# Identity and masks of an attention kernel made on GpSimd and VectorE, padding not loaded, and the order planned anew

## The chip, the cores and the metric

The program runs on one core of one Trainium2 chip. The metric is device time of one execution in microseconds; the time before is the median of three runs, 335.76 us. PE is the matrix engine TensorE, DVE is VectorE, ACT is ScalarE, POOL is GpSimd, and SP is SyncE, which here only issues DMAs.

## What is computed

Two steps follow each other, for 4 batches, 4 heads, 1088 positions. The first is an attention with a feature map (products of two projections of 8 values each, so 64 features a head). The second is a gated feed-forward block that mixes positions with a 1088 x 1088 matrix.

```python
def phi(x):
    a = np.einsum('rd,bhsd->bhsr', S1, x)
    b = np.einsum('rd,bhsd->bhsr', S2, x)
    return np.einsum('bhsi,bhsj->bhsij', a, b).reshape(*x.shape[:-1], r * r)
q_p, k_p = (phi(q), phi(k))
kv = np.einsum('bhsf,bhsd->bhfd', k_p, v)
z = np.sum(k_p, axis=2)
num = np.einsum('bhsf,bhfd->bhsd', q_p, kv)
den = np.einsum('bhsf,bhf->bhs', q_p, z)[..., None] + 1e-06
x = num / den                                   # heads side by side: 128 columns
...
h = np.maximum(x @ w_in, 0.0)                   # 1024 columns, halves u and v
v_n = (v - mean(v)) / sqrt(var(v) + 1e-06)
v_s = np.einsum('ts,bsd->btd', w_spatial, v_n) + b_spatial[None, :, None]
out = (u * v_s) @ w_out
```

## The kernel before

Positions are padded to 9 tiles of 128, in three groups of three. fp32 numbers are split into a high and a low part (wTh and wTl of w_spatial, vh and vl of the normed v, xh and xl of x, wih and wil of w_in), and three products of such parts make one full product. `S1`, `S2`, `w_in` and `w_out` arrive as fp64 bit patterns and are turned into fp32 by the seven VectorE steps of `from_f64`.

The program is a list of operations (`op`), each with its engine, its tiles and a planned cost. `Order.schedule` puts them in a row for each engine from tables of numbers: `LEADS` (how much earlier than needed an operation is due), `FORCE` (which engines may take an operation), `FIRST` (loads that go first), `T_MAIN` and `PACE` (when the products of each batch are due). In places where the plan leaves PE free it puts in products of zeros (`fill`). Each engine then works strictly in its row's order.

Batch 0 has a path of its own (`attention0`) that has to come before anything else: the table `sk` of S1 and S2 goes through `from_f64` on DVE; the keys kt are projected with it on PE; ACT copies half of that (ka), DVE multiplies the halves into features (kp), four times 128x768 for the three groups of keys and the first of queries; PE sums features and values into pu; DVE masks that by head into kd0 (L665 before); PE turns the query features with an identity matrix (L688), forms num and den (L702), DVE divides (L706 to L709), PE turns the result (L716), ACT and DVE split it into xh and xl, and `hidden_v` makes the normed v from it. Then `main` runs the large products with w_spatial (L956, L958, L965) over four column blocks d, three position chunks c, and nine tiles kt.

Before the change one array, `idn`, is loaded into `ident`: 128 columns of identity, 2 columns `in_turn` that tell the head of a pair for the kd of batches 1 to 3 (L762), and 4 columns by head for kd0 (L665). The seven steps that make `sk` need no part of it.

Of the kernel before, what the change touches and what calls it, by code (L numbers as in the profile page):

```python
# [9 lines left out]
F32 = mybir.dt.float32  # L10
# [9 lines left out]
P = 128  # L20
# [26 lines left out]
T_MAIN = (39.0, 143.0, 197.0, 292.0)  # L47
PACE = (1.145, 0.898, 1.306, 1.037)
STRETCH = 1.64
FORCE = {'abs': ['ACT'], 'norm0': ['ACT', 'DVE'], 'vl0': ['DVE'], 'v90': ['ACT'], 'W0': ['DVE'], 'W1': ['DVE'], 'W2': ['POOL']}  # L50

FIRST = ('wt21', 'wt20', 'wt02', 'wt12', 'wt11', 'wt40', 'wt01', 'wt22')
# [6 lines left out]
ON_ACT = ()  # L59
ADD_UP = 187  # L60

AHEAD = 90000
TURN = 125

SLACK = {'PE': 5, 'ACT': 29, 'DVE': 91, 'POOL': 5000, 'SP': 5000}
FILL, FILL_TO, FILL_SPARE = 224, 50.0, 150

COLD_TO, COLD = 6800, 2

FILLS = ((7000, 460, 260), (8200, 300, 100), (1e9, FILL, -FILL_SPARE))  # L70
FIRST_RATE, LOW_DELAY = 0.18, 4.4
# [48 lines left out]
class Order:  # L120
# [235 lines left out]
def c_mm(n, k=1):  # L356
    return k * max((n + 11.8) / 2.25, 111)


@with_exitstack  # L360
def tile_kernel(ctx: ExitStack, tc: tile.TileContext, kT, qT, vA, sks, idn, wT, w_in, w_out, bsp, out):
# [86 lines left out]
    def from_f64(x32, raw, n):  # L448

        def w(i):
            return raw[:, :2 * n].bitcast(U32).rearrange("p (n w) -> p w n", w=2)[:, i]

        def x():
            return x32[:, :n]

        def xb():
            return x32[:, :n].bitcast(U32)

        def step(cost, f, r, w):
            op("DVE", cost, lambda: f(nc.vector), r=r, w=w, sh=True)

        c2, c1 = c_dve2(n), c_dve(n)

        if n > NSK:
            op("ACT", c_act(n), lambda: nc.scalar.activation(x(), w(1).bitcast(F32), AF.Abs), r=[raw], w=[(x32, "x")], sh=True, alts=[("DVE", c2, lambda: nc.vector.tensor_scalar(out=xb(), in0=w(1), scalar1=0x7FFFFFFF, scalar2=None, op0=ALU.bitwise_and))], kind="abs")
        else:
            step(c2, lambda v: v.tensor_scalar(out=xb(), in0=w(1), scalar1=0x7FFFFFFF, scalar2=None, op0=ALU.bitwise_and), [raw], [(x32, "x")])
        step(c2, lambda v: v.tensor_scalar(out=x(), in0=x(), scalar1=EXP_LO, scalar2=EXP_HI, op0=ALU.max, op1=ALU.min), [], [(x32, "x")])  # L470
# [9 lines left out]
        step(c1, lambda v: v.tensor_tensor(out=x(), in0=x(), in1=ev(), op=ALU.add), [(x32, "e")], [(x32, "x")])  # L480
# [651 lines left out]
```

## Time and profile before

| what | us |
|---|---|
| median of three runs (335.5 to 335.83) | 335.76 |
| profiled execution, its own time | 335.18 |
| its span | 333.4 |
| DVE busy | 197.4 |
| ACT busy | 157.9 |
| POOL busy | 56.9 |

The span runs from the program's first instruction to its last; 1.8 us of the profiled execution's time lie around it. Times on a row of the timeline are the start from the span's start, then the duration. A timeline merges equal instructions that follow each other, with their count. In square brackets stands how long the engine was idle just before, and what ended that. In a row of windows, the figures are busy time and instructions of each engine in the stretch, then PE's granted clock, the busy share of the DMA engines and what they moved.

### The profile page before, as it was taken

The numbers are of one execution on the slowest core, as the hardware profiler recorded it, in microseconds if no ns is written. First come the engines' busy times: TensorE is split into PE (matmuls) and PEld (weight loads), VectorE is DVE, ScalarE is ACT, GpSimd is POOL, SyncE is SP. The second block draws the span as 40 slices with busy tenths as digits, with TensorE's granted clock in tenths as the row PEclk, the third lists the DMA queues.
The fourth block names the chain that finished last, engine by engine and source line by source line (L and its number), as shares of the span: only waits on it lengthen the run. The fifth ranks groups of instructions, "written<-read, shape, count | busy, mean of one in ns | idle before, by whom it ended". The sixth has DMA issues, their size and how long they took to land.

```text
span 333.4 us, 6019 instructions
## 1 busy us (share of the span) xinstructions
PE 326.5 (98%) x2304; PEld 315.4 (95%) x2304; DVE 197.4 (59%) x448; ACT 157.9 (47%) x367; POOL 56.9 (17%) x68
## 2 busy tenths in 40 slices
PE   7999999999999999999999999999999999999996
PEld 7878979999999999999999999999999999999995
DVE  4899997355889972779984232255992473121221
ACT  2589667532668652556563232336651542121212
POOL 1000105472423106401313200131000000000000
PEclk9999999999999999999999999999999999999999
DMA  7901379667310175501037110310000100000001
GB/s 210 342 20 48 109 191 316 127 135 194 86 44 27 29 123 95 118 0 48 22 54 119 42 46 0 50 31 0 3 0 2 40 27 2 0 2 0 0 2 68
DMA packets 17747, 23.09 MB, mean 69 GB/s; under 512 B 2486, under 2 KB 17462, under 8 KB 17718
## 3 DMA queue, kind: packets, MB, share of 16 engines
q1 hardware_dynamic: 17718, 22.71, 27.0%
q8 instruction: 18, 0.29, 0.4%
q14 instruction: 11, 0.09, 0.1%
HBM read 13.78 MB, written 2.23 MB: 48 GB/s over the span
## 4 chain that ended last, share of the span: by engine, by line
PE 86%; DVE 7%; ACT 2%; DMA 2%; SPq 1%; issue 1%; DVEq 0%; ACTq 0%
PE sp L956 20%; PE sp L965 18%; PE sp L958 17%; PE sd L404 3%; PE sd L405 3%; PE sd L406 3%; PE pu L404 2%; PE po L405 2%; PE pu L406 2%; PE pu L405 2%; PE sp L967 2%; PE po L406 2%; PE po L404 2%; PE sd L614 2%; DMA v<-in_vA 2%; PE sd L568 1%
## 5 line engine op out<-in xcount | busy, mean ns | idle before, releaser
L956 PE MATMUL sp<-wTh,vh 128*128 128x362 f32 (+4 forms) x414 | 135.9, 328 | 0.0
L958 PE MATMUL sp<-wTh,vl 128*128 128x362 f32 (+4 forms) x368 | 120.4, 327 | 0.0
L965 PE MATMUL sp<-wTl,vh 128*128 128x362 f32 (+4 forms) x368 | 119.0, 328 | 0.7 <-DVE wTl L533 0.7
L956 PEld LDWEIGHTS sp<-wTh,vh 128*128 128x128 f32 x414 | 78.0, 188 | 1.0
L965 PEld LDWEIGHTS sp<-wTl,vh 128*128 128x128 f32 x368 | 69.3, 188 | 1.6 <-DVE wTl L533 1.3
L958 PEld LDWEIGHTS sp<-wTh,vl 128*128 128x128 f32 x368 | 69.4, 188 | 0.7
L993 DVE TENSOR_TENSOR u<-sp,u 128x362 f32<-128x362 f32 (+3 forms) x36 | 18.4, 510 | 45.1 <-PE sp L967 44.6
L484 ACT CAST g<-u 128x362 fp32r<-128x362 f32 (+3 forms) x34 | 16.4, 482 | 38.8 <-DVE u L993 38.6
L783 DVE RECIPROCAL c<-c 128x384 f32<-128x384 f32 (+1 forms) x9 | 21.7, 2416 | 10.5 <-ACT c L781 10.5
L417 POOL TENSOR_TENSOR r<-pl,r 128x384 fp32r<-128x384 f32 (+1 forms) x18 | 17.6, 982 | 59.1 <-ACT r L484 55.1
L809 DVE BATCH_NORM_STATS2 st<-vt 128x6 f32<-128x512 f32 x36 | 24.3, 689 | 4.9 <-ACT vt L807 4.8
L414 DVE TENSOR_TENSOR g<-u,g 128x362 fp32r<-128x362 f32 (+3 forms) x34 | 19.8, 581 | 11.0 <-ACT g L484 10.9
L807 ACT ACTIVATE vt<-sd 128x512 f32<-128x512 f32 x36 | 21.4, 600 | 9.1 <-PE sd L406 8.4
L749 POOL TENSOR_TENSOR pl<-pl,pl 128x384 f32<-128x384 f32 (+1 forms) x18 | 17.6, 984 | 35.7 <-DMA pl<-abT 32.0
L417 POOL TENSOR_TENSOR r<-c,r 128x384 fp32r<-128x384 f32 (+1 forms) x9 | 10.0, 1116 | 75.5 <-ACT r L484 75.5
L885 ACT CAST vh<-vt 128x384 fp32r<-128x384 f32 x36 | 17.2, 511 | 11.3 <-PE sp L956 4.9
L948 ACT ACTIVATE u<-pu 128x362 f32<-128x362 f32 (+3 forms) x36 | 16.4, 455 | 11.0 <-PE pu L406 10.8
L993 DVE TENSOR_TENSOR kp<-sp,kp 128x424 f32<-128x424 f32 x10 | 6.0, 600 | 26.1 <-PE sp L967 26.1
L887 DVE TENSOR_TENSOR vl<-vt,vh 128x384 fp32r<-128x384 f32 (+1 forms) x36 | 17.3, 504 | 1.4 <-ACT vh L885 1.3
L404 PE MATMUL pu<-xh,wih 128*128 128x362 f32 (+4 forms) x48 | 15.9, 331 | 0.0
L406 PE MATMUL pu<-xh,wil 128*128 128x362 f32 (+4 forms) x48 | 15.8, 329 | 0.0
L405 PE MATMUL pu<-xl,wih 128*128 128x362 f32 (+4 forms) x48 | 15.7, 328 | 0.0
(166 smaller groups left out, 540.2 us busy)
## 6 DMA issues: line engine op xcount, KB each, us to landing
pl<-in_wT SPq DMA_DIRECT2D x18, 166.0 KB, 3.7
v<-in_vA SPq DMA_DIRECT2D x12, 198.0 KB, 4.0
kt<-in_kT SPq DMA_DIRECT2D x12, 192.0 KB, 3.2
pl<-abT SPq DMA_DIRECT2D x12, 192.0 KB, 3.9
pl<-in_wT SPq DMA_DIRECT2D x9, 212.0 KB, 4.7
c<-in_qT SPq DMA_DIRECT2D x9, 192.0 KB, 2.8
pl<-abT SPq DMA_DIRECT2D x24, 72.0 KB, 2.3
pl<-abT SPq DMA_DIRECT2D x6, 160.0 KB, 3.7
```

The source lines that it names most:

```text
L404: nc.tensor.matmul(o, ah, bh, start=start, stop=False)
L405: nc.tensor.matmul(o, ah, bl, start=False, stop=False)
L406: nc.tensor.matmul(o, al, bh, start=False, stop=stop)
L414: return lambda: nc.vector.tensor_tensor(out=o(), in0=a(), in1=bb(), op=ALU.subtract)
L417: return lambda: nc.gpsimd.tensor_tensor(out=o(), in0=a(), in1=bb(), op=ALU.subtract)
L783: op("DVE", 135 + 6.3 * n, lambda x32=x32, n=n: nc.vector.reciprocal(out=x32[:, :n], in_=x32[:, :n]), w=[x32])
L807: op("ACT", c_act(512, True), lambda pv=pv, t=t: nc.scalar.activation(vt[:, t], pv.ap, AF.Relu), r=[pv], w=[(vt, t)])
L809: op("DVE", 690, lambda stats=stats, t=t: nc.vector.bn_stats(out=stats.ap, in_=vt[:, t]), r=[(vt, t)], w=[stats])
L956: nc.tensor.matmul(sp[:, :cw], vh[:, kt], wTh[:, kt, cs], start=(kt == 0), stop=False)
L958: nc.tensor.matmul(sp[:, :cw], vl[:, kt], wTh[:, kt, cs], start=False, stop=False)
L965: nc.tensor.matmul(sp[:, :cw], vh[:, kt], wTl[:, kt, cs], start=False, stop=False)
L993: op("DVE", c_dve(cw), lambda: nc.vector.tensor_tensor(out=u.ap, in0=sp[:, :cw], in1=u.ap, op=ALU.mult), r=[sp], w=[u], lead=LEAD[1])
```

## The change

The array `idn` goes. POOL now fills `ident` with ones and keeps the diagonal by an `affine_select`; it makes `by_head` with three small memsets; DVE makes `in_turn` by a sum over the columns of `ident`. The padding is no longer loaded: the last 64 columns of the third group of batch 0's keys are set to zero on POOL, those of its queries are copied on POOL from the 64 columns before them, and the two loads shrink from 384 to 320 columns. `FORCE` now names engines tile by tile, and all tables of the plan have new numbers.

```diff
-T_MAIN = (39.0, 143.0, 197.0, 292.0)
-PACE = (1.145, 0.898, 1.306, 1.037)
-STRETCH = 1.64
...
-FIRST = ('wt21', 'wt20', 'wt02', 'wt12', 'wt11', 'wt40', 'wt01', 'wt22')
+T_MAIN = (2.0, 111.0, 182.0, 239.0)
+PACE = (1.537, 1.044, 1.007, 1.391)
+STRETCH = 1.24
...
+FIRST = ('wt22', 'wt21', 'wt02', 'wt12')
...
-LEAD = (8700, 7600)
...
+LEAD = (7100, 7600)
...
-SLACK = {'PE': 5, 'ACT': 29, 'DVE': 91, 'POOL': 5000, 'SP': 5000}
+SLACK = {'PE': 5, 'ACT': 175, 'DVE': 52, 'POOL': 5000, 'SP': 5000}
...
-            o.alts = tuple(a for a in o.alts if a[0] in FORCE.get(kind, [eng]))
+            o.alts = tuple(a for a in o.alts if a[0] in FORCE.get(kind, FORCE.get(kind.split(".")[0], [eng])))
...
-    ident = tl(None, "ident_sb", [P, P + 6])
-    load(ident, lambda: ident.ap, idn, 70)
+    ident = tl(None, "ident_sb", [P, P])
+    op("POOL", 260, lambda: nc.gpsimd.memset(ident.ap, 1.0), w=[ident])
+    op("POOL", 400, lambda: nc.gpsimd.affine_select(out=ident.ap, in_=ident.ap, pattern=[[-1, P]], compare_op=ALU.is_equal, fill=0.0, base=0, channel_multiplier=1), w=[ident])
+    by_head = tl(None, "by_head", [P, 2, 2])
+    op("POOL", 120, lambda: nc.gpsimd.memset(by_head.ap, 0.0), w=[by_head])
+    for a in range(2):
+        op("POOL", 120, lambda a=a: nc.gpsimd.memset(by_head[64 * a:64 * a + 64, :, a], 1.0), w=[by_head])
+    in_turn = tl(None, "in_turn", [P, 2])
+    op("DVE", 290, lambda: nc.vector.tensor_reduce(
+        out=in_turn.ap, in_=ident.ap.rearrange("p (g a i) -> p a g i", a=2, i=R), axis=mybir.AxisListType.XY, op=ALU.add,
+    ), r=[ident], w=[in_turn])
...
     def load_keys(b, g):
         xt = tl("kt", f"kt{b}{g}", [P, 384])
-        load(xt, lambda: xt.ap, kT[b, g], 192, after=AFTER[b])
+        n = 384
+        if not b and g == 2:
+
+            n = 320
+            op("POOL", 240, lambda: nc.gpsimd.memset(xt[:, n:], 0.0), w=[(xt, 1)])
+        load(xt, lambda: xt[:, :n], kT[b, g, :, :n], n // 2, w=(xt, 0), after=AFTER[b])
...
-            in1=ident[:, P + 2:].unsqueeze(2).broadcast_to([P, 4, D + 1]), op=ALU.mult,
-        ), r=[kv, ident], w=[kd0])
+            in1=by_head.ap.rearrange("p r a -> p (r a)").unsqueeze(2).broadcast_to([P, 4, D + 1]), op=ALU.mult,
+        ), r=[kv, by_head], w=[kd0])
...
-            load(xt, lambda xt=xt, g=g: xt.ap, qT[b, g], 192)
+            n = TW[g]
+            load(xt, lambda xt=xt, n=n: xt[:, :n], qT[b, g, :, :n], n // 2, w=(xt, 0))
+            if n < 384:
+
+                op("POOL", 250, lambda xt=xt, n=n: nc.gpsimd.tensor_copy(out=xt[:, n:], in_=xt[:, n - 64:n]), r=[(xt, 0)], w=[(xt, 1)])
```

How the rows of the engines move, at three places. First the start of POOL's row. `v` of L441 and L442 are the four tiles of ones for the bias, `r` of L417 the low parts of later queries, and the row ISA of L417 is in the trace two instructions MODIFY_POOL_CONFIG on POOL's sequencer. Before:

```order
L1128 UNCONDITIONAL_BRANCH
L441 CAST v_74<-z_67 64x128
L441 CAST v_78<-z_67 64x128
L441 CAST v_82<-z_67 64x128
L441 CAST v_84<-z_67 64x128
L417 ISA
L417 TENSOR_TENSOR r_660<-c_94,r_522 128x384
```

Now, with the kt of L613 the zeroed padding of the keys:

```order
L1146 UNCONDITIONAL_BRANCH
L499 MEMSET ident_sb 128x128
L500 ISA
L500 AFFINE_SELECT ident_sb<-ident_sb 128x128
L502 MEMSET by_head 128x4
L504 MEMSET by_head 64x2 x2
L613 MEMSET kt 128x64
L442 CAST v_88<-z_69 64x128
L442 CAST v_92<-z_69 64x128
```

The ISA pair has moved from the end of the small casts, ahead of the first TENSOR_TENSOR, to the second place of the row, ahead of the AFFINE_SELECT that completes `ident`; the casts stand behind it.

Second, the start of DVE's row, where `sk` is made and the first features kp are multiplied. Before:

```order
L444 MEMSET eps 128x1
L422 MEMSET z_67 128x128
L423 MEMSET z_67 2x128
L469 TENSOR_SCALAR sk<-pl_70 128x64
L470 TENSOR_SCALAR sk<-sk 128x64
L472 TENSOR_SCALAR sk<-sk 128x64
```

Now:

```order
L445 MEMSET eps 128x1
L423 MEMSET z_69 128x128
L424 MEMSET z_69 2x128
L506 TENSOR_REDUCE in_turn<-ident_sb 128x2
L470 TENSOR_SCALAR sk<-pl_65 128x64
L471 TENSOR_SCALAR sk<-sk 128x64
```

The sum that makes `in_turn` from `ident` stands ahead of the seven steps of `sk`.

Third, DVE where batch 0's last vl and the low parts wTl of w_spatial are made (L916 and L935 are vl, L533 and L543 wTl, L414 and L415 wil, L925 and L944 the low part of the last half tile; the steps on v are `from_f64`). Before:

```order
L916 TENSOR_TENSOR vl<-vt_210,vh 128x512
L925 TENSOR_TENSOR vh<-vt_210,vh 64x512
L916 TENSOR_TENSOR vl<-vt_210,vh 128x512
L533 TENSOR_TENSOR wTl<-pl_136,wTh 64x424
L533 TENSOR_TENSOR wTl<-pl_167,wTh 128x424
L533 TENSOR_TENSOR wTl<-pl_187,wTh 128x424
L414 TENSOR_TENSOR wil<-v,wih 128x512
L533 TENSOR_TENSOR wTl<-pl_208,wTh 128x424
```

Now:

```order
L543 TENSOR_TENSOR wTl<-pl_171,wTh 128x424
L935 TENSOR_TENSOR vl<-vt_214,vh 128x512
L543 TENSOR_TENSOR wTl<-pl_222,wTh 128x424
L468 TENSOR_SCALAR v<-kt 128x512
L543 TENSOR_TENSOR wTl<-pl_234,wTh 128x424
L944 TENSOR_TENSOR vh<-vt_214,vh 64x512
L935 TENSOR_TENSOR vl<-vt_214,vh 128x512
```

Three wTl stand ahead of the last vl now, wil has been done before, and an absolute value (L468) that ACT made before stands among them. In the whole stretch DVE makes 7 wTl of 424 columns rather than 9, 6 vl rather than 8 and 3 norms (L845, now L864) rather than 4; POOL and ACT make the others. PE's row has the same products; those of the attention of batches 1 to 3 come earlier in it (the last of `hidden_v` of batch 3 at row 1122 of 1760, before at row 1378 of 1761).

More of the change, by code (lines that the diff above doesn't have):

```diff
@@ L360, in tile_kernel @@
 @with_exitstack
-def tile_kernel(ctx: ExitStack, tc: tile.TileContext, kT, qT, vA, sks, idn, wT, w_in, w_out, bsp, out):
+def tile_kernel(ctx: ExitStack, tc: tile.TileContext, kT, qT, vA, sks, wT, w_in, w_out, bsp, out):
     nc = tc.nc
@@ L466, in from_f64 @@
         if n > NSK:
-            op("ACT", c_act(n), lambda: nc.scalar.activation(x(), w(1).bitcast(F32), AF.Abs), r=[raw], w=[(x32, "x")], sh=True, alts=[("DVE", c2, lambda: nc.vector.tensor_scalar(out=xb(), in0=w(1), scalar1=0x7FFFFFFF, scalar2=None, op0=ALU.bitwise_and))], kind="abs")
+            op("ACT", c_act(n), lambda: nc.scalar.activation(x(), w(1).bitcast(F32), AF.Abs), r=[raw], w=[(x32, "x")], sh=True, alts=[("DVE", c2, lambda: nc.vector.tensor_scalar(out=xb(), in0=w(1), scalar1=0x7FFFFFFF, scalar2=None, op0=ALU.bitwise_and))], kind=f"abs.{x32.name}")
         else:
@@ L533, in low @@
             return lambda: eng.tensor_tensor(out=wTl[:n, kt, cs], in0=raw[:n, :cw], in1=wTh[:n, kt, cs].bitcast(F32), op=ALU.subtract)
-        op("POOL", c_pool(cw), low(nc.gpsimd), r=[raw, (wTh, (kt, c))], w=[(wTl, (kt, c))], alts=[("DVE", c_dve(cw), low(nc.vector))], sh=True, kind=f"W{c}")
+        op("POOL", c_pool(cw), low(nc.gpsimd), r=[raw, (wTh, (kt, c))], w=[(wTl, (kt, c))], alts=[("DVE", c_dve(cw), low(nc.vector))], sh=True, kind=f"W{c}.{kt}")
     def load_bias():
@@ L761, in part @@
                     src = v[:, :, D:].broadcast_to([P, 2, D]) if den else v[:, :, :D]
-                    nc.vector.tensor_tensor(out=kd[:, 1 + pr if den else 3 * pr], in0=src, in1=ident[:, P:P + 2].unsqueeze(2).broadcast_to([P, 2, D]), op=ALU.mult)
-                op("DVE", 215, part, r=[kv, ident], w=[(kd, (pr, den))])
+                    nc.vector.tensor_tensor(out=kd[:, 1 + pr if den else 3 * pr], in0=src, in1=in_turn.ap.unsqueeze(2).broadcast_to([P, 2, D]), op=ALU.mult)
+                op("DVE", 215, part, r=[kv, in_turn], w=[(kd, (pr, den))])
         kvh, kvl = tl("kvh", f"kvh{b}", [P, 2, P], F32R), tl("kvl", f"kvl{b}", [P, 2, P], F32R)
@@ L848, in act @@
                 nc.scalar.activation(vt[:, t], vt[:, t], AF.Identity, bias=nm[:, t:t + 1], scale=rs[:, t:t + 1])
-            op("DVE", c_dve2(DH, True), dve, r=[mv, rs, nm], w=[(vt, t)], sh=True, alts=[("ACT", c_act(DH, ptr=True), act)], kind=f"norm{b}")
+            op("DVE", c_dve2(DH, True), dve, r=[mv, rs, nm], w=[(vt, t)], sh=True, alts=[("ACT", c_act(DH, ptr=True), act)], kind=f"norm{b}.{3 * g + t}")
     def main(b, st):
@@ L916, in low @@
                     return lambda: eng.tensor_tensor(out=all_d(ls), in0=x(), in1=all_d(hs).bitcast(F32), op=ALU.subtract)
-                op("DVE", c_dve(DH), low(nc.vector), r=[(vt, t), *((h, kt) for h in hs)], w=[(l, kt) for l in ls], sh=True, alts=[("POOL", c_pool(DH), low(nc.gpsimd))], kind="vl0")
+                op("DVE", c_dve(DH), low(nc.vector), r=[(vt, t), *((h, kt) for h in hs)], w=[(l, kt) for l in ls], sh=True, alts=[("POOL", c_pool(DH), low(nc.gpsimd))], kind=f"vl0.{kt}")
             else:
@@ L921, in split_t @@
                     vx = hl[d][2]
-                    op("ACT", c_act(P), lambda d=d, vx=vx: nc.scalar.copy(out=vx[:64], in_=vt[:64, t, d * P:(d + 1) * P]), r=[(vt, t)], w=[(vx, "data")], alts=[("POOL", 400, lambda d=d, vx=vx: nc.gpsimd.tensor_copy(out=vx[:64], in_=vt[:64, t, d * P:(d + 1) * P]))], kind="v90")
+                    op("ACT", c_act(P), lambda d=d, vx=vx: nc.scalar.copy(out=vx[:64], in_=vt[:64, t, d * P:(d + 1) * P]), r=[(vt, t)], w=[(vx, "data")], alts=[("POOL", 400, lambda d=d, vx=vx: nc.gpsimd.tensor_copy(out=vx[:64], in_=vt[:64, t, d * P:(d + 1) * P]))], kind=f"v90.{d}")
                 def low9(eng):
                     return lambda: eng.tensor_tensor(out=all_d(hs, slice(64, P)), in0=vt[64:, t].rearrange("p (d m) -> p d m", d=ND), in1=all_d(hs, slice(64, P)).bitcast(F32), op=ALU.subtract)
-                op("DVE", c_dve(DH), low9(nc.vector), r=[(vt, t)], w=[(h, kt) for h in hs], sh=True, alts=[("POOL", c_pool(DH), low9(nc.gpsimd))], kind="vl0")
+                op("DVE", c_dve(DH), low9(nc.vector), r=[(vt, t)], w=[(h, kt) for h in hs], sh=True, alts=[("POOL", c_pool(DH), low9(nc.gpsimd))], kind=f"vl0.{kt}")
         def out_mm(d, c, hi, lo, parts):
```

11 lines of the change are left out of this document (5 added, 6 removed).

## Prediction

> **What bounds the kernel now.** I began with the busy shares on the page, then took windows, to see where PE is not full.
>
> ```profile
> PE 326.5 (98%) x2304; PEld 315.4 (95%) x2304; DVE 197.4 (59%) x448; ACT 157.9 (47%) x367; POOL 56.9 (17%) x68
> ...
> 0.00:11.66 11.66, 9.49 (x150) 8.83 (x152) 5.87 (x15) 3.13 (x8) 1.21 (x8) 1.00 0.79 253
> 11.66:30.00 18.34, 17.45 (x133) 14.70 (x134) 17.91 (x53) 16.01 (x38) 0.00 (x0) 1.00 0.35 121
> 30.00:50.00 20.00, 19.34 (x100) 18.13 (x99) 19.70 (x46) 14.31 (x31) 1.01 (x1) 1.00 0.45 125
> 50.00:100.00 50.00, 50.00 (x421) 48.61 (x420) 31.76 (x63) 26.98 (x66) 22.77 (x23) 1.00 0.59 150
> 100.00:150.00 50.00, 50.00 (x384) 48.54 (x384) 35.25 (x82) 28.73 (x70) 14.18 (x16) 1.00 0.33 65
> ...
> 200.00:250.00 50.00, 50.00 (x354) 48.94 (x353) 29.82 (x63) 23.71 (x52) 7.22 (x9) 1.00 0.08 14
> ```
>
> PE is busy 98% of the span, and from 50 us on it has no gap at all (50.00 of 50.00 in each stretch), with the clock at 1.00. That work is the same before and after, so the end moves only by when the full stretch can begin. The gaps lie ahead of 50 us, where the attention of batch 0 and the splits have to be done; there DVE is the full engine (17.91 of 18.34, then 19.70 of 20.00). PE's own waits say little, since the plan fills its longest gap with products of zeros:
>
> ```profile
> PE sp L965 <- DVE wTl L533: 0.7, 1, 0.7
> PE sd L404 <- ACT vt L807: 0.5, 1, 0.5
> ...
> PE pu L614 <- DMA v<-in_vA: 0.3, 1, 0.3
> PE sp L716 <- DVE c L709: 0.3, 1, 0.3
> ...
> 25.27 2.34 PE L431 MATMUL po<-z 128*128 128x64 f32 x20
> ```
>
> So the chain is that of DVE from the start. Its timeline shows three anchors:
>
> ```profile
> 3.40 0.20 DVE L469 TENSOR_SCALAR sk<-pl 128x64 uint32<-128x64 uint32 x1 [2.13 <-DMA pl<-in_sks]
> ...
> 4.84 0.23 DVE L480 TENSOR_TENSOR sk<-sk 128x64 f32<-128x64 f32 x1
> 6.08 3.90 DVE L576 TENSOR_TENSOR kp<-ka,sd 128x768 f32<-128x768 f32 x4 [1.01 <-ACT ka L573]
> 10.72 0.30 DVE L665 TENSOR_TENSOR kd<-pu,ident_sb 128x132 f32<-128x132 f32 x1 [0.74 <-PE pu L614]
> 11.66 0.43 DVE L470 TENSOR_SCALAR vt<-vt 128x512 f32<-128x512 f32 x1 [0.64 <-ACT vt L467]
> ...
> 14.20 0.17 DVE L706 TENSOR_SCALAR sm<-sp 128x12 f32<-128x12 f32 x1
> ```
>
> DVE waits 2.13 us for the table of S1 and S2 and starts on it at 3.40. The four feature products end at 6.08 + 3.90 = 9.98, that is 6.58 us after the start on `sk`. DVE is idle for 0.74 and 0.64 us around the mask (L665), and from 11.66 on it has no slack up to the products with w_spatial. Whatever comes late at 11.66 comes late at the end, one for one.
>
> **The change, part by part.** I sum up against the profiled execution: its span of 333.4 us and 1.8 us around it make 335.18. The median of the three runs is 0.58 above that, and I put the sum on the median at the end.
>
> *Fewer bytes and one DMA less.* The load of `idn` (67 KB) and 32 KB each of keys and queries go.
>
> ```profile
> 4.97 0.43 SPq L411 DMA_DIRECT2D vt<-in_w_in  x1
> ...
> v<-in_vA SPq DMA_DIRECT2D x3, 198.0 KB, 5.1
> ...
> vt<-in_w_in SPq DMA_DIRECT2D x1, 512.0 KB, 6.0
> kt<-in_w_in SPq DMA_DIRECT2D x1, 512.0 KB, 6.4
> ...
> ident_sb<-in_idn SPq DMA_DIRECT2D x1, 67.0 KB, 3.4
> pl<-in_sks SPq DMA_DIRECT2D x1, 64.0 KB, 2.2
> ```
>
> In SP's row one issue of 0.43 us goes, and 99 KB ahead of the load of w_in; at 253 GB/s (first window) 99 KB are 0.4 us. w_in, issued at 4.97 and landed 6.0 later, would land some 0.4 us earlier, and so would the last v. The loads of SP are otherwise the same, with that of S1 and S2 moved to the front. This gain counts only if DVE waits for these loads, as it does now at 11.66.
>
> *Identity and masks on POOL and DVE.* In the order POOL fills `ident`, then has the pair ISA, then the affine_select; DVE has the sum for `in_turn` **ahead of the steps on `sk`**. Each engine is in order, so the steps on `sk`, and behind them all features, PE's first products and ACT's copies, wait until the affine_select is done. Nothing covers that. What POOL does before:
>
> ```profile
> 1.34 1.01 POOL L441 CAST v<-z 64x128 fp32r<-64x128 f32 x4 [0.90 <-DVE z L423]
> 38.60 1.01 POOL L417 TENSOR_TENSOR r<-c,r 128x384 fp32r<-128x384 f32 x1 [36.25 <-ACT r L484]
> ...
> L417 POOLq MODIFY_POOL_CONFIG  x2: 18/18/18, 2.3 to 2.3; - x2
> ...
> 0.73 1.28 ACT L436 ACT_TABLE_LOAD   x1 [0.73 <-PEq L1120]
> ```
>
> The memset of 128x128 is priced by the small casts, 1.01 / 4 = 0.25 us, from about 0.7 on (where ACT's first row begins): done at 0.95. The affine_select lies between such a cast, 0.25, and the TENSOR_TENSOR of 384 columns, 1.01; a third of that is 0.34, and I take 0.4. The three memsets and four casts behind it hold nobody up that the affine_select doesn't.
>
> The pair is the open price. Before, it issued at 2.3 us, 0.018 us each, and POOL did its next work only at 38.60, so the trace would hide what the pair starts. By its name it changes what POOL is set up to run; if it brings code in for the instruction behind it, that comes from memory, so the nearest rows are transfers and another engine's table load: ACT_TABLE_LOAD took 1.28 us, a load took 2.2 us from issue to landing at the least (sks), and up to 6.4 in the stream that followed (the second half of w_in). Lower end: one short transfer, 2.2. Upper end: two of the slowest, 12.7. I take 1.28 for the first of the pair and 6.4 for the second, **7.6 us**, since the stream of the first loads runs beside it. Then `ident` stands at 0.95 + 7.6 + 0.4 = 9.0, the sum for `in_turn` (priced by the mask L665, 0.30) ends at 9.3, `sk` starts about 9.35, and the features end 6.58 later, at 15.9, when every load named above has landed.
>
> [...]
>
> *Behind the features.* The absolute value for w_in on DVE (0.43, as L470) and the mask (0.30) follow at once: 15.9 + 0.46 + 0.3 = 16.7, where DVE stood at 11.66. **That is 5.0 us later**; the division at 14.20 is then 5.0 later too.
>
> *Engines chosen anew.* Between there and the last wTl of the first chunk the order takes two wTl, two vl and one norm off DVE, and adds two absolute values and one wTl of 332 columns.
>
> ```profile
> 36.54 1.00 DVE L845 TENSOR_SCALAR vt<-vt,mv,sm 128x512 f32<-128x512 f32 x2
> ...
> 38.05 0.69 DVE L916 TENSOR_TENSOR vl<-vt,vh 128x512 fp32r<-128x512 f32 x1
> 38.77 1.40 DVE L925 TENSOR_TENSOR vh<-vt,vh 64x512 fp32r<-64x512 f32 x1
> ...
> 42.94 1.09 DVE L533 TENSOR_TENSOR wTl<-pl,wTh 128x424 fp32r<-128x424 f32 x2
> ```
>
> Off: 2 x 0.55 + 2 x 0.69 + 0.50 = 3.0. On: 2 x 0.43 and at most 0.55, 1.4. DVE has some 1.6 us less to do, so PE's wait for wTl, 0.7, should go. At best all of PE's waits after 14 us go (0.7 + 0.5 + 0.3 = 1.5). At worst POOL takes it back: the 64x512 at 38.77 took 1.40 beside POOL's 38.60 to 39.61, and equal work beside no POOL 0.69; two vl now run on POOL, and two such stalls cost 2 x 0.7 = 1.4. I take -0.7, the one row that the moved work names. The zero and copied paddings of 64 columns on POOL are 0.25 each by the casts; they stand behind `by_head` in POOL's row and are done long before PE reaches the third group, if the affine_select is.
>
> Sum: +5.0 - 0.7 = +4.3; 335.18 + 4.3 = 339.5, on the median **340.1 us**.
>
> **The rivals.**
>
> *The pair costs nothing, or its code is there already.* Its place is the same, POOL's row at 0.95; its price is anything below the 2.3 us up to which loads, not `sk`, set the pace. For it speaks that both rows take 0.018 us; against it, that in both kernels the pair stands right ahead of the first TENSOR_TENSOR or AFFINE_SELECT and not ahead of the casts and memsets, so it serves those instructions. `ident` is then done at 1.4, ahead of the landing of S1 and S2, DVE waits for w_in as now, 0.4 earlier, and with -0.7 the kernel takes 334.7. Between: the features end at the price plus 8.3 us (15.9 - 7.6), the load of w_in lets DVE go on at about 10.6, so a delay begins at 2.3 us, and the gains are used up at about 3.3 (11.66 + 0.7 - 8.3 - 0.76). Above that the kernel is slower.
>
> *The plan collides later as well.* Batches 1 to 3 are pulled forward in PE's row, from a last stage at row 1378 to 1122 of 1760, so DVE's work of 31.76, 35.25 and 29.82 us in 50 us must go into a shorter time. PE takes it in order, and a stage that comes late stops it. The longest DVE step there is the reciprocal:
>
> ```profile
> L783 DVE RECIPROCAL c<-c 128x384 f32<-128x384 f32 (+1 forms) x9 | 21.7, 2416 | 10.5 <-ACT c L781 10.5
> ```
>
> One such step waited for in full, 2.4 us, gives 342.5. Against it speaks that PE has not waited once after 50 us and DVE has 15 us free in its fullest stretch.
>
> **How the numbers follow.** The end moves by the price less 3.3 us, on the median. The forecast is a price of 5.1 (the load of v) to 12.7 us; with the bounds of the plan it reaches from 336.8 to 347.3 (5.1 - 2.6 - 1.5 and 12.7 - 2.6 + 1.4 on 335.76), and has 0.73. The pair for nothing has 0.13. Prices around the turning point, 2.6 to 5.1 us, have 0.06 and give mostly no measurable change (0.2% of 335.76 is 0.7 us, about what a measurement can tell). The collision on top has 0.08. So faster 0.13, same 0.06, slower 0.81. The range 336.0 to 344.5 leaves out the pair for nothing, part of the turning point and the forecast's upper tail (a price over some 11.4 us, 0.04).
>
> **What would show it.** In the profile after: POOL's AFFINE_SELECT near 8.6 us, with idle time before it that no row explains; DVE's sum right behind; the first step on `sk` at 9 to 10 rather than at 3.4; the four features ending near 16; no wait of PE for wTl, and still none after 55 us. If AFFINE_SELECT starts at 1 us and `sk` at 3, the price was nothing and the forecast falls. If `sk` starts late but the end does not move by as much, DVE's chain had slack that I did not see.

## The result, and the profile after

| | us |
|---|---|
| before, median of 11 runs (334.63 to 336.76) | 335.55 |
| after, median of 11 runs (336.56 to 341.27) | 339.52 |
| ratio, with its 95% interval | 1.0112 [1.0080, 1.0143] |
| after, profiled execution: own time, span | 340.77, 339.1 |

The changed kernel is about 4 us slower, near the number forecast, but not for the reason forecast. The page of the kernel after, its first rows and its granted clock in forty slices of the span (each digit in tenths, 9 is 90% or more):

```profile
PE 330.3 (97%) x2302; PEld 316.9 (93%) x2302; DVE 204.5 (60%) x447; ACT 158.5 (47%) x364; POOL 65.2 (19%) x80
...
PEclk9999997899999999999999999999999999999999
```

Seventh and eighth slice, about 51 to 68 us: there TensorE did not have its full clock. Before, every window that the prediction shows had it at 1.00.

The start first, where the prediction put the loss. The timeline of after, POOL and DVE (start, duration, engine, line, operation):

```profile
0.81 0.21 POOL L499 MEMSET ident_sb<- 128x128 f32 x1 [0.29 <-POOLq L1138]
1.09 0.29 POOL L500 TENSOR_SCALAR_AFFINE_SELECT ident_sb<-ident_sb 128x128 f32<-128x128 f32 x1
...
1.42 0.29 DVE L506 TENSOR_REDUCE in_turn<-ident_sb 128x2 f32<-128x128 f32 x1
2.61 0.20 DVE L470 TENSOR_SCALAR sk<-pl 128x64 uint32<-128x64 uint32 x1 [0.91 <-DMA pl<-in_sks]
...
7.56 2.90 DVE L586 TENSOR_TENSOR kp<-ka,sd 128x768 f32<-128x768 f32 x3 [0.68 <-ACT ka L583]
10.80 0.43 DVE L468 TENSOR_SCALAR vt<-vt 128x512 uint32<-128x512 uint32 x1 [0.35 <-DMA vt<-in_w_in]
...
11.35 0.41 DVE L471 TENSOR_SCALAR vt<-vt 128x512 f32<-128x512 f32 x1
13.74 0.17 DVE L725 TENSOR_SCALAR sm<-sp 128x12 f32<-128x12 f32 x1
```

The AFFINE_SELECT begins 0.07 us after the memset ahead of it ends (0.81 + 0.21 = 1.02), and the table `sk` is begun at 2.61, earlier than before (3.40). The step on w_in stands at 11.35 (before 11.66), the division at 13.74 (before 14.20): the start is 0.3 to 0.5 us **faster**.

The loss lies after 50 us. Rows of windows, first of before, then of after; each gives the stretch, its length, the busy time of PE, PEld, DVE, ACT and POOL with instructions, PE's granted clock, DMA share and GB/s:

```profile
50.00:54.60 4.60, 4.60 (x26) 4.50 (x25) 4.42 (x9) 2.25 (x7) 2.42 (x2) 1.00 0.97 291
54.60:61.40 6.80, 6.80 (x43) 6.73 (x42) 3.47 (x6) 6.37 (x17) 4.64 (x6) 1.00 0.83 230
```

```profile
50.00:54.60 4.60, 2.73 (x14) 2.00 (x12) 4.60 (x4) 2.81 (x7) 3.84 (x6) 1.00 0.89 264
54.60:61.40 6.80, 5.86 (x17) 5.56 (x18) 2.73 (x5) 2.20 (x5) 0.43 (x1) 0.50 0.59 139
61.40:100.00 38.60, 38.60 (x358) 37.62 (x358) 22.75 (x42) 17.48 (x44) 15.16 (x16) 1.00 0.49 111
```

PE did 14 products where it had done 26, then 17 where it had done 43, the second time at a clock of **0.50**. DVE is busy for 4.60 of 4.60 us, yet with 4 instructions in place of 9. The timeline of after says which. `kp` here is the gated product u * v_s of column blocks 0 and 1, in the code g000 and g010; ACT makes the high part, DVE the low part (L415), into buffers named xh and xl; PE's output product `po` (L406) waits for each low part. First DVE, then POOL, then PE:

```profile
50.88 1.21 DVE L415 TENSOR_TENSOR xh<-kp,xh 128x424 fp32r<-128x424 f32 x1
52.01 3.47 DVE L415 TENSOR_TENSOR xl<-kp,xl 128x424 fp32r<-128x424 f32 x1
...
51.58 0.89 POOL L941 CAST v<-vt 64x128 fp32r<-64x128 f32 x2
52.45 2.58 POOL L543 TENSOR_TENSOR wTl<-pl,wTh 128x332 fp32r<-128x332 f32 x3
...
52.15 0.46 PE L406 MATMUL po<-xh,woh 128*128 128x424 f32 x1 [0.46 <-DVE xh L415]
...
52.84 0.35 PE L405 MATMUL po<-xl,woh 128*128 128x424 f32 x1
55.54 0.72 PE L406 MATMUL po<-xl,woh 128*128 128x424 f32 x1 [2.35 <-DVE xl L415]
```

The same subtraction takes 3.47 us here. Before, it took 0.59:

```profile
55.61 0.59 DVE L414 TENSOR_TENSOR xl<-kp,xl 128x424 fp32r<-128x424 f32 x1
```

Now POOL has five instructions in its row without a pause, two casts and three subtractions for wTl, and the DVE instruction ends 0.45 us after the last of them (52.01 + 3.47 = 55.48, and 52.45 + 2.58 = 55.03). PE waits 0.46 and 2.35 us, and from 54.59 us on, with the second wait still under way, the clock is at 0.50 until 61.42, where the product of 128x424 takes 0.56 to 0.72 rather than 0.36 us. These 6.83 us at half clock cost 3.4. Waits and half clock add up to 6.2 us, a little more than the 5.7 us by which the profiled span is longer. That the earlier start and other small differences give the rest back is inferred, not shown.

The 11 runs fall into three groups. By their mean clock they had no half-clock period (336.56, 337.38, 338.02; clock 0.999 to 1.0), one (339.06 to 339.99; 0.993 to 0.995) or two (340.60, 340.77, 341.27; 0.988). A period of 3.41 us (half of the 6.83) at half clock costs 1.7 us and lowers the mean by 0.005, which is how the groups are told apart; 8 of the 11 runs had at least one.

Two executions ran disturbed, at a mean clock of 0.559 and 0.657 (545.19 us in the run with 22 products below, 456.18 us of the kernel before, timed with the second run of ready subtractions on POOL); the ratios leave them out.

### The profile page after: what moved, and what is told of

The parts are those of the page before. It is cut to its first block, busy times and chain, and to the rows that moved or that the text cites. A ratio compares the mean times of both kernels' runs of the same rounds, so it can differ in the third digit from the quotient of the medians.

```text
span 339.1 us, 6008 instructions
## 1 busy us (share of the span) xinstructions
PE 330.3 (97%) x2302; PEld 316.9 (93%) x2302; DVE 204.5 (60%) x447; ACT 158.5 (47%) x364; POOL 65.2 (19%) x80
## 4 chain that ended last, share of the span: by engine, by line
PE 75%; DVE 15%; DMA 4%; ACT 3%; SPq 1%; issue 1%; DVEq 0%; ACTq 0%
PE sp L975 18%; PE sp L977 16%; PE sp L984 16%; PE sd L405 3%; PE sd L406 3%; PE sd L407 3%; PE po L406 2%; DVE st L828 2%; PE po L407 2%; DMA pl<-in_wT 2%; PE sp L986 2%; PE pu L405 2%; PE pu L407 2%; PE pu L406 2%; PE sd L629 2%; PE po L405 2%
## 5 line engine op out<-in xcount | busy, mean ns | idle before, releaser
L415 DVE TENSOR_TENSOR g<-u,g 128x362 fp32r<-128x362 f32 (+3 forms) x34 | 20.8, 612 | 8.5 <-ACT g L485 7.5
L418 POOL TENSOR_TENSOR r<-pl,r 128x384 fp32r<-128x384 f32 (+1 forms) x18 | 18.5, 1038 | 28.0 <-ACT r L485 28.0
L904 ACT CAST vh<-vt 128x384 fp32r<-128x384 f32 x36 | 18.0, 511 | 12.1 <-DVE vt L864 6.7
L906 DVE TENSOR_TENSOR vl<-vt,vh 128x384 fp32r<-128x384 f32 (+1 forms) x36 | 19.3, 543 | 2.4 <-ACT vh L904 2.0
L418 POOL TENSOR_TENSOR r<-c,r 128x384 fp32r<-128x384 f32 (+1 forms) x9 | 11.1, 1234 | 43.2 <-ACT r L485 43.2
L540 ACT CAST wTh<-pl 128x332 fp32r<-128x332 f32 (+1 forms) x27 | 12.7, 500 | 7.5 <-DMA pl<-in_wT 7.2
```

The source lines that it names most:

```text
L415: return lambda: nc.vector.tensor_tensor(out=o(), in0=a(), in1=bb(), op=ALU.subtract)
L418: return lambda: nc.gpsimd.tensor_tensor(out=o(), in0=a(), in1=bb(), op=ALU.subtract)
```

## The experiments

Each experiment takes one of the two kernels as planned, and edits `order`, the finished list of all operations, just before the code is put out from it. Nothing else in the plan moves. `at` finds an operation in the list, `move(a, b)` puts a right behind b; `Fill` is an operation of its own. Each ratio is to the kernel before on the same chip. The theory to be tested, in the expectations the collision: POOL's run of instructions holds DVE's low part, PE waits for that, and the wait halves the clock. The rivals are named in each expectation.

**PE's waiting products later.** In the kernel after, the two waiting groups of `po` are put behind products that need neither of the two late low parts. DVE's and POOL's rows stay.

```diff
+move("po00:1", "sp030:13")
+move("po00:2", "sp030:18")
```

> The changed kernel, with only two things moved: the two products into po (L405 to L407, of chunk 0, slices 0 and 1) that TensorE waited at stand later in TensorE's own order, the first behind four more L984 products, the second behind the eight L984 and L986 products of slice 3. VectorE's and GpSimd's orders are as in the changed kernel. Theory A (the loss is TensorE's wait for xh and xl at 52 to 55 us, and the half clock that follows it): VectorE's L415 into xl still takes about 3.5 us, but no wait of TensorE over 0.6 us is left at 51 to 56 us, the granted clock stays at 1.00, and the time falls by some 5.5 to 6 us from the profiled 340.8, to 333.8 to 335.2, a ratio to the kernel before of 0.995 to 0.999. Theory B (the clock falls at 54.6 us for a reason other than the wait): the wait's 3 us go, the clock still shows 0.50, about 337.5. Theory C (the loss lies elsewhere in the new plan or in the start): no change, 339.5.

Measured: 336.52 us, ratio 1.0024 [1.0011, 1.0037], clock 0.999 to 1.0. The DVE row and the windows of this kernel:

```profile
51.51 3.50 DVE L415 TENSOR_TENSOR xl<-kp,xl 128x424 fp32r<-128x424 f32 x1
...
50.00:54.60 4.60, 4.60 (x27) 4.51 (x26) 4.60 (x4) 2.24 (x6) 4.29 (x6) 1.00 0.82 253
54.60:61.40 6.80, 6.12 (x33) 4.87 (x32) 4.99 (x10) 3.80 (x9) 0.95 (x1) 1.00 0.59 144
```

The hold is there as in the kernel after, 3.50 us, and costs PE nothing in the first window, since other work lies there. Some 3 of the 4.0 us are back. Some 0.9 us are left, so the time lies above the 333.8 to 335.2 us expected; in the second window PE still misses 0.7.

**PE kept busy in the wait.** The kernel after, with products of zeros put ahead of the second waiting group: 22 in one run, 11 in the other.

```diff
+i = at("po00:2")
+order[i:i] = [Fill(lambda: fill("sp", 0)) for _ in range(22)]  # 11 in the second
```

> The changed kernel with 22 products of zeros (128x64, into a bank of PSUM that is free then) put ahead of the second waiting product into po, so that TensorE works while it would wait for xl. Nothing else moves; the product itself comes no earlier. Theory A (the idle time of 2.4 to 2.7 us is what halves the clock): the granted clock stays at 1.00, TensorE's idle time there is under 0.6 us, and about 3 us of 340.8 go: 336.6 to 338.2, as the fastest runs of the changed kernel, ratio 1.003 to 1.008. Theory B (the clock falls for another reason): the clock still shows 0.50 for some 7 us, 339.5 to 341.

> The changed kernel with 11 products of zeros (0.228 us each, as the 22 showed, so 2.5 us in all) ahead of the second waiting product into po: TensorE works while it would wait for xl, and holds nothing up where xl is as late as in the changed kernel's profile. Theory A: clock 1.00 in all runs, TensorE's product into po begins no earlier than 55 us, and the time is that of the changed kernel less the half clock's 3 us: 336.8 to 338.2. Theory B (the clock falls anyway): 0.50 for some 7 us in most runs, 339.5 to 341.

With 22: 339.67 us (5 runs), 1.0121 [1.0100, 1.0141], clock 0.999 to 1.0. The dose was wrong: I had counted 0.11 us for each product, and they took 0.228, 5.02 us in all, longer than the wait they were to fill. With 11: 337.86 us, 1.0068 [1.0046, 1.0089], clock 0.998 to 1.0 in all. DVE, PE and the window of the run with 11:

```profile
51.73 3.46 DVE L415 TENSOR_TENSOR xl<-kp,xl 128x424 fp32r<-128x424 f32 x1
...
52.54 2.56 PE L432 MATMUL sp<-z 128*128 128x64 f32 x22
...
54.60:61.40 6.80, 6.80 (x43) 6.58 (x43) 4.67 (x10) 3.90 (x9) 0.58 (x2) 1.00 0.59 143
```

Each fill is two rows of the trace, hence x22. The hold is the same and PE's useful work is as late as in the kernel after, but PE is not idle, and the clock stays at 1.00. The profiled executions are 337.38 against 340.77, the 3.4 us of two half-clock periods. So it is the **idleness** of PE that halves the clock here, not the load at that place, and the half clock is a cost beside the wait. The run with 22 adds one observation: its subtraction for xl came through in 1.00 us, and the DVE row behind it, a wTl of 64x332 and two more, was held instead: 4.18 us for the three, beside the same run on POOL, where the three took 1.32 in the kernel after.

**POOL's three subtractions on DVE.** In the kernel after, the wTl:15, 14 and 24 keep their places in the list and are issued by VectorE.

```diff
-nc.gpsimd.tensor_tensor(out=wTl[:, kt, cs], ...)
+nc.vector.tensor_tensor(out=wTl[:, kt, cs], ...)   # for wTl:15, wTl:14, wTl:24
```

> The changed kernel with GpSimd's three L543 subtractions at 52.45 us (wTl, 128x332) on VectorE, each emitted at the same place of the order, so behind xl. [...] Rival (xl is late because of its operands, or because of VectorE's own queue): it still ends near 55 us, and the time stays at 339 to 341.

336.08 us, 1.0010 [0.9996, 1.0023], clock 0.998 to 1.0. DVE's and POOL's rows and the first window:

```profile
51.01 1.09 DVE L415 TENSOR_TENSOR xl<-kp,xl 128x424 fp32r<-128x424 f32 x1
52.03 1.09 DVE L543 TENSOR_TENSOR wTl<-pl,wTh 64x332 fp32r<-64x332 f32 x2
...
50.34 1.31 POOL L418 TENSOR_TENSOR r<-c,r 128x320 fp32r<-128x320 f32 x1 [1.00 <-ACT r L485]
51.60 1.16 POOL L941 CAST v<-vt 64x128 fp32r<-64x128 f32 x2
...
50.00:54.60 4.60, 4.60 (x25) 4.27 (x25) 3.42 (x6) 2.38 (x6) 2.42 (x3) 1.00 0.92 279
```

Without the three, hold, wait and half clock are gone, though DVE now has more to do (3.42 us busy, no longer all of the window). By the theory it would have been 333.8 to 335.5 us, with 0.6 to 1.5 for the subtraction into xl; the time lies 0.6 above that, the subtraction within. By what path POOL's instructions hold DVE, no run shows. The low part's 1.09 us begin beside POOL's L418, ahead of the casts. The wTl at 52.03 begins 0.43 us into the first cast, as xl did in the kernel after (52.01 against 51.58), and it and the one merged with it take 1.09 us together: here the casts without subtractions behind them held nothing up for long.

**The start alone.** The kernel before with its order untouched, and only the start of the change: identity and masks on POOL and DVE, padding made on POOL, the three loads gone or shorter.

```diff
-load(ident, lambda: ident.ap, idn, 70)
+nc.gpsimd.memset(ident[:, :P], 1.0)
+nc.gpsimd.affine_select(out=ident[:, :P], in_=ident[:, :P], pattern=[[-1, P]], compare_op=ALU.is_equal, fill=0.0, base=0, channel_multiplier=1)
+nc.gpsimd.memset(by_head, 0.0)   # and two memsets of 64x2
+nc.vector.tensor_reduce(out=ident[:, P:P + 2], in_=..., axis=mybir.AxisListType.XY, op=ALU.add)
...
+nc.gpsimd.memset(kt02[:, 320:], 0.0), nc.sync.dma_start(out=kt02[:, :320], in_=kT[0, 2, :, :320])
+nc.gpsimd.tensor_copy(out=qt02[:, 320:], in_=qt02[:, 256:320])
```

> The kernel before, its order kept, with the first half of the change alone: identity, masks and sums made by GpSimd and VectorE at the start, and the padding of the last keys and queries of batch 0 not loaded (a memset and a copy on GpSimd instead). Theory A (this half costs nothing and lets the first loads land a little earlier): AFFINE_SELECT begins near 1 us, the first step for sk at 2.6 to 3.4 us, and 334.9 to 335.4 us against 335.5, ratio 0.998 to 1.000. Rival 1 (the pair of configuration instructions ahead of AFFINE_SELECT costs 6 to 8 us in runs that no profile shows): 339 to 341. Rival 2 (the start is where the changed kernel gains nothing, and the masks cost a few tenths): 335.7 to 336.2.

335.05 us, **0.9977 [0.9963, 0.9990]**: this half of the change makes the kernel faster, by 0.6 us. POOL's and DVE's rows:

```profile
0.81 0.20 POOL L1090 MEMSET ident_sb<- 128x128 f32 x1 [0.29 <-POOLq L1139]
1.09 0.29 POOL L1091 TENSOR_SCALAR_AFFINE_SELECT ident_sb<-ident_sb 128x128 f32<-128x128 f32 x1
...
3.52 0.20 DVE L469 TENSOR_SCALAR sk<-pl 128x64 uint32<-128x64 uint32 x1 [1.83 <-DMA pl<-in_sks]
```

Here too the AFFINE_SELECT starts at 1.09, and DVE goes on waiting for S1 and S2, not for POOL.

**A collision made in the kernel before, by POOL.** POOL's wTl:21 done four times, beside DVE's two low parts.

```diff
+i = at("wTl:21")
+order[i:i] = [Fill(order[i].fn)] * 3
```

> The kernel before, with one thing added: GpSimd's first L533 subtraction after 54 us (wTl, 128x332) is done four times over instead of once, the same result each time, so that GpSimd is busy without a break for some 3.6 us beside VectorE's L414 into xh and xl, as in the changed kernel. Theory A (an unbroken run of GpSimd's keeps VectorE's L414 out): one of the L414 at 54.7 to 55.6 us takes 2 to 4 us where it took 0.6 to 1.0, TensorE waits 1.5 to 3 us for it at 56 us, and the time is 1.5 to 3 us longer, or 4.5 to 6 where the clock falls as well: 337 to 342. Rival (VectorE and GpSimd run side by side, and xl was late in the changed kernel for another reason): L414 keeps its 0.6 to 1.0 us, and the time stays within 0.5 us of 335.5.

336.16 us, 1.0020 [1.0004, 1.0036]. POOL and DVE:

```profile
54.59 4.40 POOL L533 TENSOR_TENSOR wTl<-pl,wTh 128x332 fp32r<-128x332 f32 x4 [1.07 <-ACT wTh L530]
...
54.99 1.03 DVE L414 TENSOR_TENSOR xh<-kp,xh 128x424 fp32r<-128x424 f32 x1 [0.19 <-ACT xh L484]
55.95 1.30 DVE L414 TENSOR_TENSOR xl<-kp,xl 128x424 fp32r<-128x424 f32 x1
```

A miss: the low parts took 1.03 and 1.30, not 3.5. DVE came through between POOL's instructions, and POOL's were longer in turn (1.10 each, where the three in a row of the kernel after took 0.86 each).

**A late low part, made by repeating it on DVE.** In the kernel before, DVE makes the low part g010 seven times, or four times. POOL's row stays as it is.

```diff
+i = at("g010:2")
+order[i:i] = [Fill(order[i].fn)] * 6   # 3 in the second
```

> The kernel before, with VectorE's L414 into xl at 55.6 us done seven times over instead of once (the same result each time), so that TensorE's product into po at 56.57 us waits for it until 59.2 us, some 2.7 us. GpSimd's work is as before. Theory A (a wait of TensorE of this length halves the granted clock for some 7 us after it): 0.50 shows in the record from about 59 us on, and the time is the wait's 2.7 us and some 3 us more: 340.5 to 342. Theory B (the half clock in the changed kernel had another cause than the wait): the clock stays at 1.00 and the time is 2.5 to 3 us longer, 338 to 338.7.

> The same with VectorE's L414 into xl done four times over, a wait of TensorE of about 1.1 us. Theory A with a limit between 1.1 and 2.5 us: the clock stays at 1.00, and the time is 1.0 to 1.4 us longer, 336.5 to 337. Theory A without a limit (every wait halves the clock): 0.50 for several us, 339 to 340.5.

342.49 us, 1.0205 [1.0173, 1.0237], and 340.86 us, 1.0156 [1.0125, 1.0186]. PE's wait was longer than meant in both, since one subtraction took 0.87 us on average with seven and 1.05 with four, and not 0.6 (xh, just before, took 1.24 in the run with four, beside POOL's subtraction of 53.92 to 55.11): 5.0 where 2.7 was meant, 3.1 where 1.1 was. So the lower limit of the wait was not tried. Waits and windows, of the run with seven, then of that with four:

```profile
61.70 0.72 PE L405 MATMUL po<-xl,woh 128*128 128x424 f32 x1 [4.97 <-DVE xl L414]
...
54.20:57.60 3.40, 2.52 (x15) 2.15 (x13) 3.06 (x5) 3.40 (x10) 2.22 (x3) 1.00 1.03 347
57.60:61.00 3.40, 0.00 (x0) 0.00 (x0) 3.30 (x4) 1.04 (x3) 2.24 (x2) 1.00 0.51 122
61.00:67.80 6.80, 6.10 (x21) 6.00 (x22) 2.23 (x5) 2.35 (x6) 2.75 (x3) 0.50 0.30 54
```

```profile
59.73 0.72 PE L405 MATMUL po<-xl,woh 128*128 128x424 f32 x1 [3.09 <-DVE xl L414]
...
55.40:58.80 3.40, 1.24 (x7) 0.86 (x6) 3.30 (x5) 2.79 (x8) 2.62 (x3) 1.00 0.89 313
58.80:65.60 6.80, 5.87 (x20) 5.79 (x21) 2.49 (x4) 2.36 (x6) 3.02 (x4) 0.50 0.38 65
```

The kernel before, too, falls to half clock for 6.8 us at such a wait, so the fall belongs to the wait and not to the new plan.

**Ready subtractions on POOL in the kernel before, twice.** First wTl:12, 18 and 19 are taken from DVE and put on POOL behind `ql11`, so that they stand ready one after the other; later, with wTl:20 as well and `ql11` done twice, so that POOL's run lies over both low parts. They test the theory in its general form, that any such run holds DVE (A' where an expectation has letters).

```diff
-nc.vector.tensor_tensor(out=wTl[:, kt, cs], ...)
+nc.gpsimd.tensor_tensor(out=wTl[:, kt, cs], ...)   # wTl:19, 18, 12; in the second also wTl:20
+move(name, "ql11:1")                               # 19, 18, 12
...
+order.insert(i, Fill(order[i].fn))                  # the second: i = at("ql11:1")
```

> The kernel before with three of VectorE's L533 subtractions at 51 us (wTl, 128x332, three different tiles, all ready) on GpSimd instead, behind its L417 of 51 us, so that GpSimd has four of them in a row from about 53 us. The earlier try with one subtraction repeated left gaps of 0.08 us between GpSimd's instructions, and VectorE came through at each. Theory A' (VectorE is kept out as long as GpSimd's next instruction stands ready): one VectorE subtraction at 53 to 55 us takes 2 us or more, TensorE waits 1 to 2 us for xh or xl near 56 us, and the time is 1 to 2.5 us longer, more where the clock falls: 336.5 to 340. Rival (VectorE comes through between any two of GpSimd's instructions): no VectorE instruction there over 1.4 us, and 335 to 336.2, since VectorE has 1.3 us less to do.

> The kernel before with four of VectorE's L533 subtractions (wTl, 128x332 three times and 64x332) on GpSimd, behind its L417 of 51 us, which is done twice so that the four start near 53 us and stand ready one behind another until 57 us, when VectorE's L414 into xh and xl come (54.7 us). In the run with three on GpSimd its fourth instruction was not ready when the third ended, and VectorE came through there. Theory A' (VectorE is kept out as long as GpSimd's next instruction stands ready): the L414 into xh takes 2 us or more, TensorE waits 1.5 to 2.5 us for it near 56 us, the time is 2 us longer or, where the clock falls, 4 to 5: 337 to 340.5. Rival (it comes through between any two instructions, and xl's 3.5 us in the changed kernel needs something else): no L414 over 1.4 us, 335.5 to 336.7.

336.16 us, 1.0020 [1.0000, 1.0040], and 335.49 us, 0.9993 [0.9975, 1.0011]. POOL and DVE of the first, then of the second:

```profile
54.30 2.21 POOL L533 TENSOR_TENSOR wTl<-pl,wTh 128x332 fp32r<-128x332 f32 x1
...
53.82 0.90 DVE L533 TENSOR_TENSOR wTl<-pl,wTh 64x332 fp32r<-64x332 f32 x1
54.65 0.58 DVE L414 TENSOR_TENSOR xh<-kp,xh 128x424 fp32r<-128x424 f32 x1
55.16 0.59 DVE L414 TENSOR_TENSOR xl<-kp,xl 128x424 fp32r<-128x424 f32 x1
```

```profile
53.06 4.21 POOL L1101 TENSOR_TENSOR wTl<-pl,wTh 128x332 fp32r<-128x332 f32 x4
...
54.21 1.06 DVE L414 TENSOR_TENSOR xh<-kp,xh 128x424 fp32r<-128x424 f32 x1 [0.25 <-ACT xh L484]
55.20 1.32 DVE L414 TENSOR_TENSOR xl<-kp,xl 128x424 fp32r<-128x424 f32 x1
```

Both miss (one run of the first had 339.01 us at a clock of 0.993, as with one half-clock period; there is no profile of it). In the first it is POOL that is held, 2.21 us for a subtraction of 0.9, while DVE's xh and xl run at full speed (0.58 and 0.59). In the second the two engines take turns. A run of ready subtractions on POOL alone is therefore not enough to hold DVE, and the theory in that general form falls.

**What remains of the new plan's cost.** Two attempts. One takes the kernel after with the three subtractions on DVE, and puts four more operations of ACT, POOL's input and PE in another order, to remove the small waits that were left. The other takes the start alone and moves wTl:6, 7, 18 and 19 on DVE, to remove a wait for wTl of 0.7 us.

```diff
+ahead("u010:1", "wTh:16")
+move("qh10:1", "u010:1")
+ahead("u030:1", "wTh:23")
+move("po10:1", "kab30:1")
```

```diff
+move("wTl:6", "wTl:5")
+move("wTl:7", "wTl:15")
+move("wTl:18", "g010:2")
+move("wTl:19", "wTl:18")
```

> The changed kernel with the waits that are left in it taken away by order alone: the three L543 of 52.45 us on VectorE (as before), ScalarE's cast of the first queries of batch 1 later, so that GpSimd's L418 does not stand beside VectorE at 39 us, two of ScalarE's L967 ahead of casts that wait for a DMA, and the product into po at 123 us behind the keys of batch 2. If the sum of the waits (0.5 at 41, 0.2 at 46, 0.45 at 55, 0.5 at 123 us) is what the new plan still costs beside the run with the three on VectorE (336.1): 334.5 to 335.2, ratio 0.997 to 0.999. If new collisions take their place: 335.6 to 336.5.

> The kernel before with the start of the changed kernel, as in the run of the start alone, and four of VectorE's subtractions for wTl in another order: those of chunk 0, for which TensorE waits 0.7 us at 45 us, before the steps for w_out, and two of chunk 1 behind the products xh and xl. If that wait is worth what it shows and nothing is late in its place: TensorE's wait for wTl goes, 334.0 to 334.6 us, ratio 0.995 to 0.997. If the next thing is late instead (xh and xl at 55 us, or a buffer of the loads of w_spatial that comes free later): 334.8 to 335.6.

The first: 335.32 us, 0.9989 [0.9978, 1.0001], so about 0.7 us of what the new plan still cost was a matter of order; the time is 0.1 above the range expected. The second: 336.44 us, 1.0026 [1.0013, 1.0039]. It is no fair test: wTl:18 and 19 (low parts of w_spatial, tiles 6 and 7 of the second chunk) came to stand behind the next loads into their buffers, so they were made from the next tiles and waited 1.99 us for those. The wait for wTl went, and PE waited 1.0 us for xh and 0.8 for kp instead.

**The budget**, from the medians, each less that of the kernel before timed with it, beside the step from the row above:

| kernel | less before, us | step |
|---|---|---|
| start of the change alone | -0.57 | -0.6 |
| whole change, three subtractions on DVE | +0.46 | +1.0, the new plan without the collision |
| whole change, wait filled with 11 products | +2.40 | +1.9, the collision's wait |
| whole change | +3.97 | +1.6, the half clock |

The fastest version found is the start of the change alone, 0.9977 of before with all of the interval below 1.

## Why the prediction came out as it did

The time lies in the range and the sign is right, but the main step fell, and the loss came from a term that was priced too small. That the number agrees is luck: the +5.0 was nothing, and the new plan, priced at -0.7, cost some 4.5 (3.97 + 0.57, from the budget). The sentence "the end moves only by when the full stretch can begin" took for granted that the new order keeps PE as full as the old one did.

*Fewer bytes.* Right in size: w_in's step moved from 11.66 to 11.35, of the 0.4 us forecast.

*The pair of MODIFY_POOL_CONFIG, the term of +5.0.* **This step failed.** The text had put its own test: if the AFFINE_SELECT starts at 1 us and `sk` at 3, the price was nothing. They start at 1.09 and 2.61 in the kernel after, at 1.09 and 3.52 in the start alone. I went from "this issues ahead of such instructions" to "this brings code in", and took 7.6 us from transfers that have nothing to do with it. The rows had 0.018 us for each of the pair before and 0.012 after, and no profile shows any price beyond that; nor do the 12 runs of the start alone, all between 334.21 and 335.65 us. The 7.6 us were an estimate that no run shows. The rival "the pair costs nothing" was right about the mechanism, with a chance of 0.13, but its 334.7 left out what was to come after 50 us. For the start by itself, its sum without the -0.7 of the new plan would have been 335.4, and 335.05 was measured.

*Between 2.3 and 3.3 us of price the start's slack is used up.* Not tried, as the price was nothing. What can be seen is that the four features end at 10.46 (7.56 + 2.90), 0.5 later than before, for want of `ka`, and still nothing behind them is later, as w_in lands last.

*Engines chosen anew, -0.7, at worst +1.4 for stalls on POOL.* **Here the loss arose.** PE's wait for wTl did go, as forecast. The bound took the trace's one stall (1.40 against 0.69) and counted it twice. One such stall was measured at 2.9 us (3.47 against 0.59); that is the term mis-sized first. The second omission is that a wait of PE cost more than itself here: half a clock for 6.83 us, 3.4 us in the profiled execution, which no row of before showed, since before had no such wait.

*"PE has not waited once after 50 us and DVE has 15 us free in its fullest stretch."* This was said against the rival of a later collision, with 0.08, and it was the sentence that misled. It is a mean over 50 us. At 52 us DVE had an instruction for which PE waits, beside a full run on POOL. The rival named the right kind of event, but a reciprocal of 2.4 us as its price; the wait was of that size (2.35), by another mechanism, and the half clock came on top.

*No wait of PE after 55 us.* Wrong, as the wait ends at 55.54; behind it PE was full again (38.60 of 38.60 from 61.4 to 100).

What is **shown**: taking POOL's three subtractions away removes hold, wait and half clock at once; covering the wait with other products leaves the hold and removes the half clock; a wait made by repeats on DVE brings the half clock to the kernel before. What is **open**: why POOL's run holds DVE to its end at this place. All four traces with it (the kernel after, the later products and both fills) have two casts and three ready subtractions on POOL, and a DVE subtraction that begins 0.43 or 0.44 us into the first cast. The casts alone do not do it: from the same place two of DVE's subtractions took 1.09 us together in the run with the three on DVE, and one took 0.68 in the run with four more operations reordered. Nor do subtractions alone: beside four in a row DVE's took 1.06 and 1.32, and 63 low parts on DVE that have a row of their own and begin inside a TENSOR_TENSOR of POOL, in the timelines of the 14 kernels (of the kernels before and after the whole span, of the others mostly the first 15 us and some 50 to 62), took 1.43 us at most. So the hold goes with both together in these traces; whether the casts ahead of the subtractions decide it wasn't tried.

## What to carry to other kernels

Where a new plan puts GpSimd instructions in a row beside a VectorE instruction for which TensorE waits, as the subtraction into xl was (3.47 us against 0.59), look at that one place and not at means over a stretch; a stall seen once is no upper bound. Add to a wait of TensorE what the clock may cost on top: 2.35 us after 0.46 cost 3.5 us on the median here (3.97 - 0.46), 3.1 cost 5.4, and 5.0 cost 7.0. Put other ready products there, or products of zeros if there are none. Split a change into its parts with the order frozen: here half of it paid 0.6 us, and the other half hid that.

## What the runs showed of the hardware

**The clock fell by periods.** In the trace of the kernel after the granted clock is, from 6.80 us on, 1.0 for 47.79 us, 0.50 for 6.83, and 1.0 for 276.48; in that of the kernel before it is, from 4.94 us on, 1.0 for 327.68. These are 14, 2, 81 and 96 times 3.413 us, so a period of 3.413 us is my estimate from them. The windows of such single periods show what PE did in the one before the fall, here in the kernel after:

```profile
51.18:54.59 3.41, 1.55 (x7) 0.84 (x5) 3.41 (x2) 1.95 (x5) 3.41 (x6) 1.00 0.91 281
54.59:58.00 3.41, 2.46 (x7) 2.32 (x8) 2.14 (x4) 0.47 (x1) 0.44 (x1) 0.50 0.36 98
58.00:61.42 3.42, 3.42 (x12) 3.26 (x11) 0.60 (x1) 1.75 (x4) 0.00 (x0) 0.50 0.83 179
```

PE was idle for 1.9 of 3.41 us (3.41 - 1.55), and the next period is at half clock; that one has 0.95 idle and the one after it none, and the clock is back only behind a period that was full. With the low part made four times, 2.2 of 3.40 us were idle ahead of the fall; with seven, 0.9 idle (54.20 to 57.60) did not bring it, and the fully idle period behind it did. At the ends of the runs, where PE's work runs out, it fell behind a period with 1.96 us idle (334.48 to 337.89 in the kernel after, PE busy for 1.45) and behind one with 2.45 (329.21 to 332.62 in the kernel before, busy for 0.96). So in these traces 0.9 us idle in one period left the clock at 1.00 and 1.86 did not; where between them it turns is not shown. Whether the clock falls would then depend on how a wait lies against the periods; that is an estimate, and it fits that the same kernel had none, one or two of them from run to run. Two timed runs of the kernel before (338.03 us at 0.994, 336.88 at 0.995) look as if they had one, too; there is no profile of them. Of the 11 runs of the kernel after, whose profiled one waited 2.35 us after 0.46 there, 8 had a fall by their mean clock (0.988 to 0.995).

**VectorE was held over several GpSimd instructions, and the reverse.** Beside one instruction of POOL the subtraction into xl took 1.09 us in the run with the three on DVE (51.01, POOL's L418 from 50.34 to 51.65), where 0.59 is the time alone (55.61 in the kernel before). In the kernel after, the one at 52.01 did not end with the casts beside which it began, at 52.47; it ended at 55.48, behind all of POOL's run. Elsewhere the engines took turns (1.06 and 1.32), or POOL was the one held: 2.21 us against 0.9, and in the kernel before 2.14 for the L417 at 51.04 (1.01 at 38.60), beside four subtractions of DVE in a row (50.47 to 52.30). Who goes next, when both have an instruction ready, no run here settles.
